# Loading q and k so that neighbouring partitions hold neighbouring token pairs

## The chip, the cores and the metric

The kernel runs on one core of one Trainium2 chip. The metric is the device time of one execution in microseconds (us), and the median over the runs is compared. A core has five engines with queues of their own: PE (TensorE, matrix products), DVE (VectorE), ACT (ScalarE), POOL (GpSimd) and SP (SyncE, which here only issues transfers). Each engine works through its own instructions in order. Sixteen DMA engines move data between the device memory and the on-chip memory of 128 partitions.

## The reference

The program is sliding-window attention followed by a gated feed-forward layer:

```
q, k, v: [8 batches, 8 heads, 576 tokens, 64]   float32
scores = q k^T / 8 + bias,  bias = -slope[h] * |i - j|,  only 0 <= i - j < 128
attn   = softmax(scores);   a = attn v
x      = a as [4608 tokens, 512]
H = max(x w_h, 0);  T = sigmoid(x w_t + b_t)
out    = T * H + (1 - T) * x                     [4608, 512] float32
```

## The kernel before

**Tiles.** A batch has eight heads in two groups `g` of four. Its 576 tokens go through four stages `s` of 128 queries; the last 64 tokens of two batches share a fifth block. The first half of the program is attention: for each batch and group, q and k are loaded (`load`, L150), transposed on DVE (`tr`, L231), multiplied on PE (`scores`, L263), put through the exponential on ACT (`soft`, L277), multiplied by a mask on DVE (`mask`, L283 to L287) and multiplied by v on PE (`pv`, L309). `norm` (L319, L320) on DVE divides by the sums. The second half takes the result `x` of a block, transposes it on PE (L329), copies it (L334), multiplies it by the two weight matrices (L347, L386), and forms the gate: `uu` (L356), tanh (L398), scaling of `tt` on ACT or DVE (L406, L408), the products and sums of L364, L417 and L424 on POOL or DVE, and the store on SP (L430).

**The load of q and k.** For batch `b`, group `g` and kind q or k, one transfer issued by POOL brings four heads of 576 tokens into the tile `LD[b % 2, g, kind]`, 128 partitions of 18 x 64 bf16, and casts from float32 on the way. The pattern is `"h (s t) d -> (h s) (t d)"` with t = 18: partition 32h + s holds tokens 18s to 18s + 17 of head h, one run of 4608 bytes in the device memory and of 2304 on the chip. There are 32 such loads, two sets of tiles in turn, so that a load of batch b + 2 comes behind the transpose of batch b in the same tile. v has a load per batch (L156) of 4608 pieces of 64 values, and SP copies half of v across partitions (`vo`, L172). Where the profile writes `ld11k`, the first digit is `b % 2`, the second `g`.

**The transpose.** DVE's transpose works on blocks of 32 x 32. A token's 64 bf16 values are read as 32 words of 4 bytes, so one block is 32 partitions by one token index t: it reads 32 words of one token index from each partition, and writes, into a partition per word, 32 values that lie 18 words (72 bytes) apart. Its output tile `TR` has, in partition 32h + i, word i of every token of head h in token order, and `scores` reads the even and the odd value of each word through its last index `e`.

**The order.** The program's order is a string, ORDER, of three-character steps, a letter for the function and two digits for the place in its list (`lists()`); each engine's queue has its steps in that order. `L` is a load of q or k, `T` a transpose, `V` a load of v, `G`, `g`, `o` and `O` the gates and adds on POOL and DVE. On POOL the loads of q, k and v stand between gates (L417) and adds (L424), and an issue takes POOL's own time. A transpose waits for its load, an issue on POOL waits for the transpose that last read its tile, and an issue waits for an earlier transfer with the same semaphore, of which POOL has eight in turn.

Of the kernel before, what the change touches and what calls it, by code (L numbers as in the profile page):

```python
# [9 lines left out]
P = 128  # L10
NB, NS, NG, NH = 8, 4, 2, 4
NP, NP3, NT, NVO = 5, 3, 18, 4
SPIN = 22
FILL = {(0, 1): 2, (0, 2): 2, (0, 3): 2, (1, 0): 2, (1, 1): 2}
SIG = {(3, 4), (7, 0), (7, 1), (7, 2), (7, 3)}
# [58 lines left out]
def kernel(  # L74
# [10 lines left out]
    nc = tc.nc  # L85
    B, H, S, D = q.shape
# [6 lines left out]
    U32 = mybir.dt.uint32  # L93
# [18 lines left out]
    LD = {(i, g, w): cp.tile([P, NT * D], BF16, name=f"ld{i}{g}{w}")  # L112
          for i in range(2) for g in range(NG) for w in "qk"}
    TR = {(i, g, w): cp.tile([P, SQ, 2], BF16, name=f"tr{i}{g}{w}")
          for i in range(2) for g in range(NG) for w in "qk"}
# [23 lines left out]
    def between(ins, last=None):  # L139
        last = last or paired[0]  # L140
        if last is not None:
            tc.add_manual_dep(
                ins.ins, last.name,
                mybir.DependencyInfo(mybir.DependencyClass.Sync, mybir.DependencyReason.DATA),
                reason="starts behind an operation of VectorE")

    def load(kind, *at):
        if kind in "qk":
            b, g = at
            nc.gpsimd.dma_start(  # L150
                out=LD[b % 2, g, kind][:],
                in_=(q if kind == "q" else k)[b, 4 * g : 4 * g + 4].rearrange(
                    "h (s t) d -> (h s) (t d)", t=NT))
        elif kind == "v":
            b, = at
            ins = nc.gpsimd.dma_start(  # L156
                out=va[:, b, :, 0:D],
                in_=v[b].rearrange("h s d -> (h s) d").rearrange("(n p) d -> p n d", p=P))
            if scaled[0] is not None:
                between(ins, scaled[0])  # L160
        elif at[0] < 2:
            nc.gpsimd.dma_start(
                out=(wH, wT)[at[0]][:],
                in_=(moe_w_h, moe_w_t)[at[0]].rearrange("(c p) n -> p c n", p=P))
        else:
            nc.gpsimd.dma_start(
                out=bT[0:1, :], in_=moe_b_t.rearrange("(o n) -> o n", o=1))
# [60 lines left out]
            nc.scalar.copy(out=MK[:, :, 1, 192:256], in_=MK[:, :, 0, 0:D])  # L228

    def tr(w, b, g):  # L230
        ins = nc.vector.transpose(  # L231
            out=TR[b % 2, g, w][:, 0:S].rearrange("p s e -> p (s e)").bitcast(U32).rearrange(
                "p (s t) -> p t s", t=NT),
            in_=LD[b % 2, g, w][:].bitcast(U32).rearrange("p (t i) -> p t i", i=32))
        if b == 0:
            turned[0] = ins.ins

    def warm():
        ps = take(1)[:, 0, :]
        for _ in range(SPIN):  # L240
            nc.tensor.matmul(out=ps, lhsT=spin[:, 0:P], rhs=spin[:], start=True, stop=True)
# [4 lines left out]
    def take(n, dtype=F32):  # L246
        i = int(next(bank))
        t = PS[:, i : i + n, :]
        return t if dtype == F32 else t.bitcast(dtype)
# [163 lines left out]
    def gate(b, s, on, half=0):  # L413
        eng, note = (nc.vector, alone) if on == "g" else (nc.gpsimd, between)
        at = cols(b, s, half)
        uu = UU[b, s][:, at]
        note(eng.tensor_tensor(out=uu, in0=uu, in1=TT[b, s][:, at], op=ALU.mult))  # L417

    def add_x(b, s, on, half=0):
        eng, note = (nc.gpsimd, between) if on == "o" else (nc.vector, alone)  # L420
        if half == 0:
            OT[b, s] = op.tile([P, DM], F32, name="ot")
        at = cols(b, s, half)
        note(eng.tensor_tensor(out=OT[b, s][:, at], in0=UU[b, s][:, at], in1=X[b, s][:, at], op=ALU.add))  # L424

    def store(b, s, half=0):
# [5 lines left out]
        for r in range(2):  # L432
# [5 lines left out]
                  q=lambda b, s, half: gate(b, s, "g", half), j=lambda b, s, half: add_x(b, s, "O", half))  # L438

    do = dict(L=load, V=load, W=load, X=lambda w, b: across(b), b=bias, T=tr, s=scores, e=soft, m=mask, p=pv, n=norm, x=x_tr, c=x_copy, h=mm_h,  # L440
              u=relu_sub, v=sub_x, z=mm_z, a=tanh, t=to_gate, g=gate, o=add_x, d=store)
    with tc.manual_schedule():
        steps = "".join(ORDER)
        for n in range(0, len(steps), 3):
# [19 lines left out]
            kind = step.lower() if step in "GOU" else {"D": "t", "N": "v"}.get(step, step)  # L464
# [30 lines left out]
```

## Time and profile before

| | |
|---|---|
| median of 3 runs | 153.02 us (151.66 to 153.88) |
| profiled execution | 151.17 us |
| its span, first to last instruction | 149.5 us |
| TensorE clock granted | 0.995 |
| PE busy | 121.4 us (81%) |
| DVE busy | 130.8 us (88%) |
| ACT busy | 120.6 us (81%) |
| POOL busy | 93.2 us (62%) |
| the 32 transposes of q and k (L231) | 4 x (5.0 us) for each of 8 tiles, 1241 to 1252 ns each in the mean |
| issue of the 32 loads of q and k (L150) | 551 to 618 ns of POOL each in the mean |
| packets of the software queue | 42688, 15.21 MB |
| packets in all | 49403, under 512 bytes 38496 |

The profile is of one execution. Busy times add up the instructions of an engine. A line of a group gives source line, engine, operation, output and input, shapes, count, then busy time and mean of one in ns, then the idle time of the engine just before them and what ended it. A line of the order in time gives start, duration, engine, source line and tiles. The waits name who waited for whom, with total, number and longest. Windows give each engine's busy time in a stretch of the span.

### The profile page before, as it was taken

To read this page: it belongs to the slowest core of one execution; us is meant where nothing else is said; L and a number is where in the kernel's file an instruction comes from. 1 tells how busy PE (TensorE), PEld (TensorE's weight loads), DVE (VectorE), ACT (ScalarE), POOL (GpSimd) and SP (SyncE) were. 2 spreads that over 40 slices of the span, in tenths; PEclk is the share of its full clock that TensorE was granted. 3 is DMA by queue.
4 is the path that set the end of the run, shared out by engine and by line. 5 is a ranking of instruction groups with operands and counts; after the bars stand their busy time and mean duration, and the time that the engine had idled before them with its cause. 6 is when DMAs were issued, how large, how long until landed. Compare 5 with 4: busy or idle time off the path is not lost.

```text
span 149.5 us, 6187 instructions
## 1 busy us (share of the span) xinstructions
PE 121.4 (81%) x2680; PEld 68.7 (46%) x2713; DVE 130.8 (88%) x248; ACT 120.6 (81%) x177; POOL 93.2 (62%) x101
## 2 busy tenths in 40 slices
PE   0008897887999897979999699968999999999940
PEld 0003544364555454554565455444555645556420
DVE  3687499997999999999999899299999999999990
ACT  3085907858799999979999899959999999999720
POOL 6990700089098986996999953918699933609030
PEclk9999999999999999999999999999999999999997
DMA  2999999999999999999979999988927996350752
GB/s 38 196 164 181 216 232 186 169 152 200 162 181 197 243 167 198 224 257 177 213 236 174 201 167 271 267 154 223 186 105 133 144 295 177 136 151 7 274 219 71
DMA packets 49403, 27.44 MB, mean 184 GB/s; under 512 B 38496, under 2 KB 39776, under 8 KB 49376
## 3 DMA queue, kind: packets, MB, share of 16 engines
q0 software_dynamic: 42688, 15.21, 96.9%
q1 hardware_dynamic: 6528, 11.71, 23.6%
q8 instruction: 21, 0.34, 1.0%
q10 hardware_dynamic: 160, 0.13, 0.3%
q14 instruction: 6, 0.05, 0.1%
HBM read 30.41 MB, written 9.44 MB: 267 GB/s over the span
## 4 chain that ended last, share of the span: by engine, by line
DMA 42%; DVE 21%; ACT 12%; POOL 7%; issue 7%; PE 6%; SPq 1%; DVEq 0%; POOLq 0%
DMA va<-in_v_dram 24%; DMA ld01k<-in_k_dram 10%; DMA vo<-va 7%; DVE x L320 5%; DVE uu L356 3%; ACT p L277 3%; POOL uu L417 2%; DVE p L283 2%; ACT tt L398 2%; PE ps L386 2%; ACT e L277 2%; ACT xt L334 2%; DVE ot L424 2%; DVE tr01q L231 2%; POOL ot L424 2%
## 5 line engine op out<-in xcount | busy, mean ns | idle before, releaser
L424 POOL TENSOR_TENSOR ot<-uu,x 128x512 f32<-128x512 bf16 x29 | 33.1, 1157 | 16.3 <-DVE uu L417 6.0
L277 ACT ACTIVATE p<-ps 128x1536 bf16<-128x1536 f32 x24 | 34.9, 1461 | 7.7 <-PE ps L263 7.4
L386 PE MATMUL ps<-wT,xt 128*128 128x512 bf16 x128 | 35.9, 380 | 1.3 <-ACT ps L377 0.3
L417 POOL TENSOR_TENSOR uu<-uu,tt 128x512 bf16<-128x512 bf16 x17 | 19.5, 1151 | 26.8 <-DVE tt L408 13.8
L347 PE MATMUL ps<-wH,xt 128*128 128x512 bf16 (+1 forms) x134 | 35.2, 373 | 1.1 <-issue 0.5
L320 DVE TENSOR_TENSOR x<-ps,rd 128x512 bf16<-128x512 f32 x36 | 24.9, 692 | 1.8
L283 DVE TENSOR_TENSOR p<-p,mk 128x1536 bf16<-128x1536 bf16 x24 | 22.5, 949 | 0.5 <-ACT p L277 0.4
L334 ACT COPY xt<-ps 128x512 bf16<-128x512 bf16 x36 | 21.2, 596 | 1.6 <-PE ps L329 1.6
L398 ACT ACTIVATE tt<-ps 128x512 f16<-128x512 f32 x31 | 18.6, 616 | 3.3 <-PE ps L386 2.7
L309 PEld LDWEIGHTS <-p 64*128 64x128 bf16 x768 | 15.2, 94 | 12.6 <-issue 11.2
L309 PE MATMUL ps<-vo,p 64*128 64x65 bf16 x384 | 17.8, 191 | 3.2 <-DMA vo<-va 2.6
L309 PE MATMUL ps<-va,p 64*128 64x65 bf16 x384 | 18.3, 191 | 1.6 <-DVE uu L356 1.4
L356 DVE SCALAR_TENSOR_TENSOR uu<-ps,x 128x512 bf16<-128x512 f32 (+1 forms) x29 | 19.1, 662 | 0.5 <-PE ps L347 0.5
L377 ACT COPY ps<-bA 128x512 f32<-128x512 f32 x32 | 19.3, 608 | 0.1
L347 PEld LDWEIGHTS <-xt 128*128 128x128 bf16 x148 | 12.7, 98 | 12.3 <-issue 1.1
L386 PEld LDWEIGHTS <-xt 128*128 128x128 bf16 x144 | 12.6, 98 | 12.3 <-issue 0.9
L263 PE MATMUL ps<-tr00q,tr00k 32*64 32x192 bf16 (+1 forms) x288 | 10.0, 254 | 10.1 <-DVE tr00k L231 9.6
L156 POOL DMA_DIRECT2D va<-in_v_dram x8 | 14.8, 1849 | 4.5 <-DMA va<-in_v_dram 4.0
L329 PE MATMUL ps<-ident,x 128*128 128x128 bf16 x144 | 13.6, 220 | 2.4 <-DVE x L320 1.4
L277 ACT ACTIVATE e<-ps 128x1792 bf16<-128x1792 f32 x8 | 13.3, 1667 | 2.4 <-PE ps L263 2.3
L263 PEld LDWEIGHTS <-tr00k 32*64 32x64 bf16 x288 | 6.7, 108 | 15.6 <-DVE tr00k L231 9.6
L329 PEld LDWEIGHTS <-x 128*128 128x128 bf16 x144 | 9.6, 97 | 9.0 <-issue 3.6
(79 smaller groups left out, 213.8 us busy)
## 6 DMA issues: line engine op xcount, KB each, us to landing
out_dram<-ot SPq DMA_DIRECT2D x32, 256.0 KB, 4.0
va<-in_v_dram POOLq DMA_DIRECT2D x8, 576.0 KB, 11.1
vo<-va SPq DMA_DIRECT2D x16, 146.2 KB, 5.8
ld00q<-in_q_dram POOLq DMA_DIRECT2D x4, 288.0 KB, 7.2
ld01k<-in_k_dram POOLq DMA_DIRECT2D x4, 288.0 KB, 5.7
ld00k<-in_k_dram POOLq DMA_DIRECT2D x4, 288.0 KB, 6.7
ld01q<-in_q_dram POOLq DMA_DIRECT2D x4, 288.0 KB, 7.3
ld11k<-in_k_dram POOLq DMA_DIRECT2D x4, 288.0 KB, 7.4
```

Source lines behind the costliest of these rows:

```text
L277: nc.scalar.activation(out=out, in_=in_, func=ACTF.Exp, scale=scale)
L283: alone(nc.vector.tensor_tensor(out=p, in0=p, in1=MK[:, :, :, 0:192], op=ALU.mult))
L309: nc.tensor.matmul(out=av[o : o + m, g, h * (D + 1) : (h + 1) * (D + 1)], lhsT=PT[bb, st][rows, h].rearrange("p i n -> p (i n)")[:, c : c ...
L320: nc.vector.tensor_tensor(out=x[:].rearrange("p (r i d) -> p r i d", i=NH, r=2), in0=av[:, :, :, 0:D], in1=rd[:].to_broadcast([P, 2, NH, D ...
L329: nc.tensor.transpose(out=pt[:, c * P : (c + 1) * P], in_=X[b, s][:, c * P : (c + 1) * P], identity=ident[:])
L334: nc.scalar.copy(out=xt[:].rearrange("p c n -> p (c n)"), in_=XP.pop((b, s)))
L347: nc.tensor.matmul(out=pa, lhsT=XT[b, s][:, c, :], rhs=wH[:, c, at], start=c == 0, stop=c == NC - 1)
L356: nc.vector.scalar_tensor_tensor(out=uu, in0=pa, scalar=0.0, in1=X[b, s][:, at], op0=ALU.max, op1=ALU.subtract)
L386: nc.tensor.matmul(out=pz, lhsT=xt[:, c, :], rhs=wT[:, c, :], start=c == 0 and not given, stop=c == NC - 1 and given, skip_group_check=given)
L398: nc.scalar.activation(out=tt[:], in_=pz, func=ACTF.Tanh, scale=0.5)
L417: note(eng.tensor_tensor(out=uu, in0=uu, in1=TT[b, s][:, at], op=ALU.mult))
L424: note(eng.tensor_tensor(out=OT[b, s][:, at], in0=UU[b, s][:, at], in1=X[b, s][:, at], op=ALU.add))
```

## The change

For batches 2 to 7 (FLAT = 2) the load and the transpose get other patterns; batches 0 and 1 keep the old ones. A token index is now split as 36a + 4c + 2j + e, with 64 values of a over the four heads, nine of c, and two each of j and e. Partition 2a + j holds the nine pairs (c; e = 0, 1), so neighbouring partitions hold neighbouring pairs of tokens. Each pair is a run of 512 bytes in the device memory and 256 on the chip. The load becomes two transfers, one for the even partitions (j = 0) and one for the odd ones (j = 1), each of 64 partitions x 9 runs. The transpose reads as before, 32 words of one token index (c, e) from each of 32 partitions, but writes them along a (36 words apart) and j (2 words apart): two words for each a, 8 bytes apart, in one aligned run of 16 bytes. The output tile holds the same values in the same places as before. Scores, the order and all else are unchanged.

```diff
+FLAT = 2
...
         if kind in "qk":
             b, g = at
-            nc.gpsimd.dma_start(
-                out=LD[b % 2, g, kind][:],
-                in_=(q if kind == "q" else k)[b, 4 * g : 4 * g + 4].rearrange(
-                    "h (s t) d -> (h s) (t d)", t=NT))
+            src = (q if kind == "q" else k)[b, 4 * g : 4 * g + 4]
+            if b < FLAT:
+                nc.gpsimd.dma_start(
+                    out=LD[b % 2, g, kind][:],
+                    in_=src.rearrange("h (s t) d -> (h s) (t d)", t=NT))
+            else:
+                src = src.rearrange("h s d -> (h s) d").rearrange(
+                    "(a c j e) d -> j a c (e d)", c=NT // 2, j=2, e=2)
+                for j in range(2):
+                    nc.gpsimd.dma_start(
+                        out=LD[b % 2, g, kind][j::2].rearrange("a (c x) -> a c x", c=NT // 2),
+                        in_=src[j])
...
     def tr(w, b, g):
+        out = TR[b % 2, g, w][:, 0:S].rearrange("p s e -> p (s e)").bitcast(U32)
+        if b < FLAT:
+            out = out.rearrange("p (s t) -> p t s", t=NT)
+        else:
+            out = out.rearrange("p (a c j e) -> p c e a j", c=NT // 2, j=2, e=2)
         ins = nc.vector.transpose(
-            out=TR[b % 2, g, w][:, 0:S].rearrange("p s e -> p (s e)").bitcast(U32).rearrange(
-                "p (s t) -> p t s", t=NT),
-            in_=LD[b % 2, g, w][:].bitcast(U32).rearrange("p (t i) -> p t i", i=32))
+            out=out, in_=LD[b % 2, g, w][:].bitcast(U32).rearrange("p (t i) -> p t i", i=32))
```

In the new kernel the load of batches 0 and 1 is line 153 and that of batches 2 to 7 line 160.

## The prediction, written before the run

> **What bounds the kernel now.** I read the page first (busy time by engine, and the chain of work that ended last), then the busy time by stage in windows, then the groups by line and shape, then the order of time on POOL around the q and k loads.
>
> ```profile
> PE 121.4 (81%) x2680; PEld 68.7 (46%) x2713; DVE 130.8 (88%) x248; ACT 120.6 (81%) x177; POOL 93.2 (62%) x101
> ...
> DMA 42%; DVE 21%; ACT 12%; POOL 7%; issue 7%; PE 6%; SPq 1%; DVEq 0%; POOLq 0%
> ```
>
> DVE is the busiest engine, POOL looks free by a third, and the chain runs through loads for 42% of the span. An average hides where POOL is free, so the next view is by stage:
>
> ```profile
> core 0: us, PE busy (x) PEld busy (x) DVE busy (x) ACT busy (x) POOL busy (x), PEclk, DMA share, GB/s
> 31.00:48.00 17.00, 15.51 (x373) 8.98 (x383) 15.70 (x26) 14.71 (x21) 12.24 (x15) 1.00 1.40 176
> 48.00:65.00 17.00, 14.52 (x327) 8.76 (x331) 16.50 (x28) 16.68 (x26) 14.90 (x15) 1.00 1.47 217
> 65.00:82.00 17.00, 16.32 (x395) 9.34 (x400) 16.47 (x27) 15.76 (x22) 15.64 (x16) 1.00 1.50 203
> 82.00:99.00 17.00, 14.05 (x292) 7.85 (x296) 13.55 (x25) 16.07 (x27) 11.02 (x12) 1.00 1.63 229
> 99.00:113.00 14.00, 13.38 (x359) 7.72 (x358) 13.72 (x25) 12.36 (x17) 10.19 (x11) 1.00 0.71 152
> ```
>
> From 31 to 82 us DVE is busy 48.67 of 51 us and POOL 42.78 of 51: POOL has 8.2 us free where the loads of batches 3 to 6 are issued, and what it has free after 113 (15.88 busy of 36.5) comes too late for any load of q or k. Issuing is POOL's own time:
>
> ```profile
> L156 POOL DMA_DIRECT2D va<-in_v_dram x8 | 14.8, 1849 | 4.5 <-DMA va<-in_v_dram 4.0 <-issue 0.5
> L150 POOL DMA_DIRECT2D ld01k<-in_k_dram x4 | 2.3, 574 | 0.0
> L162 POOL DMA_DIRECT2D wH<-in_moe_w_h_dram x1 | 0.8, 785 | 0.0
> L166 POOL DMA_DIRECT2D bT<-in_moe_b_t_dram x1 | 0.6, 573 | 0.0
> ```
>
> The mean of one issue grows with its pieces: 573 ns for bT (16 pieces, by its pattern), 574 for a q or k load (128 rows), 785 for wH (512), 1849 for v (4608). And the loads are used soon after they land:
>
> ```profile
> 67.24 0.61 POOL L150 DMA_DIRECT2D ld11k<-in_k_dram  x1
> 67.84 0.54 POOL L150 DMA_DIRECT2D ld00k<-in_k_dram  x1
> 68.36 0.55 POOL L150 DMA_DIRECT2D ld11q<-in_q_dram  x1
> ```
> ```profile
> 74.00 1.25 DVE L231 STREAM_TRANSPOSE tr11k<-ld11k 128x576 uint32<-128x576 uint32 x1
> ```
>
> POOL issues back to back; this ld11k (batch 5) lands at 73.22 by the trace and is transposed 0.8 us later. By the same reading ld11k of batch 3 has 0.02 us to spare, ld01k of batch 6 0.02, the q and k of heads 0 to 3 of batch 2 0.28 and 0.61, most others 1.4 to 8.
>
> **The change, part by part.**
>
> *Transposes.* 24 of 32 keep their 576 columns and get another output walk. Rows for the price:
>
> ```profile
> L231 DVE STREAM_TRANSPOSE tr00k<-ld00k 128x576 uint32<-128x576 uint32 x4 | 5.0, 1247 | 0.0
> L424 DVE TENSOR_TENSOR ot<-uu,x 128x512 f32<-128x512 bf16 x6 | 4.0, 685 | 0.0
> L424 DVE TENSOR_TENSOR ot<-uu,x 128x256 f32<-128x256 bf16 x2 | 0.8, 418 | 0.0
> L189 DVE MEMSET va<- 128x288 bf16 x1 | 0.3, 298 | 1.0 <-issue 1.0
> L176 DVE MEMSET bT<- 128x256 uint32 x1 | 0.3, 272 | 0.0
> ```
>
> The adds that write dense 4-byte columns take 685 - 418 = 267 ns for 256 columns, 1.04 ns each, plus 151 fixed. At that rate 576 columns cost 752 ns; the transpose takes 1247, or 1.90 ns a column. If its 72-byte output step is the reason, the change saves up to 0.50 us each, 24 x 0.50 = 12 us of DVE time. The other end is nothing: the memset of L189 steps 130 bytes between elements and takes 298 ns for 288, on the line of the dense ones (165 for 128, 272 for 256, so 299 for 288). A loss is not excluded, the walk now has four dimensions; I bound it by 0.1 us each (2.4 in all). I take 0.50, since an operation that also reads is nearer to the adds than to a memset, and keep both ends.
> The Trainium skill, SBUF — State Buffer, section "Door 1", says that SBUF has 16-byte lines and that two accesses to a line are needed for full rate. By it the saving is real, by the memset row it is nil; the sum below moves by only 1 us between them.
>
> *Issue on POOL.* 24 loads become 48, each of 64 x 9 = 576 pieces. Between wH (512, 785 ns) and v (4608, 1849) the line gives 0.80 us. A load then costs 2 x 0.80 - 0.575 = +1.03 us of POOL. Ends: flat at 0.575 each (+0.575), and 0.85 (+1.13); below nothing only if the price went with the 64 partitions, and bT on one partition costs as much as 128. I take +1.03. Two of the loads (16.8 and 17.3) stand before a 12.4 us wait of POOL and cost it nothing. The order counted from the list of issues is 8 loads in 31 to 48, 4 in 48 to 65, 4 in 65 to 82, 6 in 82 to 113. What stands behind them on POOL, in order, are the gates of L417, the adds of L424, the v loads and the next q and k loads.
>
> The ledger for POOL, 31 to 82: 42.78 + 16 x 1.03 = 59.3 us of work in 51. So POOL, with no gap at all, is 8.3 us late at 82. The loads there have 0.02 to 1.4 us to spare, so DVE waits for them, and with it PE's scores and all behind. DVE's 16 transposes of that stretch, 8 us shorter, give nothing back: DVE waits instead. From 82 to 113 POOL has 21.21 + 6 x 1.03 = 27.4 us of work in 31, and DVE 8 transposes left (4.0 us saved), but ACT is busy 28.43 of those 31; I let it win back 0.8 us. Without faster transposes it wins back none: 1 us, as said. Sum: +7.5 us.
>
> *Transfers.* In the trace's packets 1229 to 1237 of 128 bytes start each us while v flows alone, 90 to 94 of 2304 bytes: 13 and 178 ns per packet on one of 16 engines. The line between gives 22.7 ns for the new 256-byte packets. A load was 8 x 178 = 1.42 us and becomes 2 x 36 x 22.7 = 1.63: +0.2 us, 5 us in all, inside the time that POOL's lateness opens between loads; I cost it at nothing. If that cover is gone, up to 0.2 x 16 = 3.3 us by 82.
>
> *Waits.* In the kernel's list of instructions POOL's transfers signal on eight semaphores in turn, so each issue waits for the eighth transfer before it. It shows once:
>
> ```profile
> POOL va L156 <- DMA va<-in_v_dram: 4.0, 1, 4.0
> ```
>
> With 67 transfers instead of 43 that comes more often. Eight issues of 0.80 us are 6.4 us; a load lands in 5.7 to 7.8 (medians), a v load in 11.1. I cost it at nothing where POOL is late anyway, and at 4 us for the upper end. Each transpose waits for two transfers, the second 0.80 us after the first; this is in the +1.03. PE, ACT and SP keep their instructions.
>
> The Trainium skill, DMA: Bandwidth & Descriptors, section "Rules for kernel authors", speaks against the split: two transfers to disjoint halves of the partitions serialize, and one of 128 is to be used. By it alone a load would cost one more fixed issue (+0.575); the rows above already hold that.
>
> **The rivals.**
>
> - *The issue is flat.* The piece count is nothing, two issues cost 1.15 us. For it: bT and q/k at 573 and 574. Against: wH and v. Ledger: 42.78 + 16 x 0.575 = 52.0 of 51, +1.0 by 82, little won back: 152 to 155. The Trainium skill says in DMA: Bandwidth & Descriptors, "Anatomy of one DMA", that descriptor generation is small and many fit before its cost shows; that is this rival, and the v row at 1849 ns disagrees.
> - *Faster: the issue goes with the partitions.* A half then costs 0.29, a load as much as now, and the 12 us of DVE time come free. It decides from an extra of under 0.33 us per load: 42.78 + 16 x 0.33 = 48, 3 us under 51. ACT (82.4 busy in 30 to 120) and PE (81.6) would stop it after some 8 us; I take -5, 148 us. Against: bT.
> - *More waits.* The eighth-transfer wait comes on top (+4): 164.5.
> - *The change does nothing on DVE.* Transposes stay at 1247 and POOL's ledger stays: 161.5. It is inside the forecast's range.
>
> **How the numbers follow.** The profiled execution took 151.17 us (span 149.5 and 1.7 around it); the median of the runs, 153.02, is 1.85 above it. +7.5 gives 158.7 against the profiled one and 160.5 by the median; I give 160.5. Chances: POOL's issue time is the bound, transposes shorter or not, 0.66; more waits 0.14; flat issue 0.13; faster 0.07. So slower by over 2% is 0.80, within 2% 0.13, faster 0.07; 2% is about what runs from 151.66 to 153.88 can tell from no change. The forecast's own range is 156.5 to 163. The range for 8 in 10 is 155 to 165: it leaves out the faster case (0.07), most of the flat one (0.08) and the worst waits (0.05).
>
> **What would show it.** In the profile after: issues of L160 at about 0.80 us, 48 of them, and 16 of L153 as now; POOL busy 93.2 + 24 x 1.03 = 118 us and nearly all of 31 to 90; DVE idle before transposes of ld tiles, 8 us and more where it was 0.3 + 2.6 after 31 us; the transposes of batches 2 to 7 at 0.75 us, those of 0 and 1 at 1.25; packets 49403 - 24 x 128 + 48 x 576, about 74000, with the software queue's share little changed. Wrong it would be if an issue took under 0.45 us, if POOL kept free time from 31 to 82, or if DVE's waits for the loads did not grow.

## The result and the profile after

The changed kernel took 161.81 us (median of 4, 160.97 to 162.13) against 153.45 (median of 4, 151.66 to 155.27): a ratio of 1.058 with a 95% interval of 1.047 to 1.069. The profiled execution took 160.97 us, its span 159.2. Ratios here leave out executions that were disturbed by a lower granted clock, medians keep them, so that the two do not always divide exactly. All executions of the kernel before, in the rounds of the experiments too, took 151.10 to 158.19 us, less than the shortest of the changed kernel.

The page of the changed kernel, busy times:

```profile
PE 127.1 (80%) x2713; PEld 70.1 (44%) x2713; DVE 133.3 (84%) x248; ACT 121.3 (76%) x177; POOL 118.4 (74%) x125
...
DMA packets 74364, 27.45 MB, mean 172 GB/s; under 512 B 66528, under 2 KB 67808, under 8 KB 74336
...
q0 software_dynamic: 67648, 15.21, 111.3%
```

POOL went from 93.2 to 118.4 us. DVE did not become lighter, although its transposes did (below). There are 385 packets more than the 73979 of the prediction's sum; e3 below, which has the 24 transfers more but no new pieces, also has 385 more than the kernel before. The software queue's packets took 111.3% of the span of 16 engines instead of 96.9%.

The windows of the changed kernel, with the same columns as before (length, PE, PEld, DVE, ACT, POOL, clock, DMA):

```profile
31.00:48.00 17.00, 16.38 (x384) 9.41 (x384) 14.16 (x26) 14.55 (x21) 16.73 (x19) 1.00 1.68 154
48.00:65.00 17.00, 13.41 (x330) 8.14 (x331) 13.51 (x21) 13.55 (x20) 16.94 (x16) 0.90 1.71 185
65.00:82.00 17.00, 13.87 (x307) 7.66 (x306) 13.42 (x21) 12.65 (x19) 16.96 (x18) 1.00 1.54 156
82.00:99.00 17.00, 13.73 (x268) 7.67 (x269) 15.67 (x26) 14.14 (x22) 16.86 (x16) 0.90 2.01 190
```

POOL is busy 50.63 of the 51 us from 31 to 82, and full on to 99. In these 51 us every other engine is busy for less time: DVE is busy 41.09 of the 51 us where it was busy 48.67. What POOL does there is read from the groups and from the order of time on POOL:

```profile
L165 POOL DMA_DIRECT2D va<-in_v_dram x8 | 14.7, 1837 | 4.2 <-DMA va<-in_v_dram 4.2
L160 POOL DMA_DIRECT2D ld10k<-in_k_dram x6 | 4.6, 773 | 0.0
```
```profile
74.79 1.55 POOL L160 DMA_DIRECT2D ld11k<-in_k_dram  x2
76.34 1.50 POOL L160 DMA_DIRECT2D ld00k<-in_k_dram  x2
77.83 1.50 POOL L160 DMA_DIRECT2D ld11q<-in_q_dram  x2
```
```profile
111.76 0.59 POOL L150 DMA_DIRECT2D ld11q<-in_q_dram  x1
```
```profile
121.03 1.55 POOL L160 DMA_DIRECT2D ld11q<-in_q_dram  x2
```

An issue takes 756 to 773 ns in the mean of each tile, two of them 1.5 us. The three loads whose issue took from 67.24 to 68.91 us now take from 74.79 to 79.33; the last load of all (the last two views, before and after) is issued at 121.03 instead of 111.76, 9.3 us late, and the span is 9.7 us longer. The lateness at the last load is carried to the end.

DVE around 70 us, in order of time, in the kernel before with its groups for the mask and for POOL's gate, then DVE and POOL in the changed kernel:

```profile
69.81 1.25 DVE L231 STREAM_TRANSPOSE tr10k<-ld10k 128x576 uint32<-128x576 uint32 x1
70.91 0.68 DVE L356 SCALAR_TENSOR_TENSOR uu<-ps,x 128x512 bf16<-128x512 f32 x1
```
```profile
L283 DVE TENSOR_TENSOR p<-p,mk 128x1536 bf16<-128x1536 bf16 x24 | 22.5, 949 | 0.5 <-ACT p L277 0.4
L417 POOL TENSOR_TENSOR uu<-uu,tt 128x512 bf16<-128x512 bf16 x17 | 19.5, 1151 | 26.8 <-DVE tt L408 13.8
```
```profile
69.48 0.77 DVE L245 STREAM_TRANSPOSE tr01q<-ld01q 128x576 uint32<-128x576 uint32 x1
...
71.93 1.90 DVE L295 TENSOR_TENSOR p<-p,mk 128x1536 bf16<-128x1536 bf16 x1
73.76 1.50 DVE L298 TENSOR_TENSOR r<-e,mk 128x768 bf16<-128x768 bf16 x1
75.18 0.68 DVE L299 TENSOR_TENSOR r<-e,mk 128x1024 bf16<-128x1024 bf16 x1
75.78 0.77 DVE L245 STREAM_TRANSPOSE tr10k<-ld10k 128x576 uint32<-128x576 uint32 x1
76.48 0.65 DVE L368 SCALAR_TENSOR_TENSOR uu<-ps,x 128x512 bf16<-128x512 f32 x1
```
```profile
71.82 1.19 POOL L436 TENSOR_TENSOR ot<-uu,x 128x512 f32<-128x512 bf16 x1
72.98 1.86 POOL L429 TENSOR_TENSOR uu<-uu,tt 128x512 bf16<-128x512 bf16 x1
```

The new walk takes 0.77 us instead of 1.25. The records of neighbouring DVE operations overlap a little, so the order of time gains less than the 0.48: the next operation starts 1.10 us after the start of an old transpose and 0.70 after that of a new one, which is 0.40 for each and 9.6 for 24. But the mask product, 0.95 us before, takes 1.90 here, and the next 1.50 instead of 0.55: they run while POOL, behind its time, does an add and a gate, and the gate is stretched too (1.86 for 1.15). Counted over the trace, 16 of the bf16 products of DVE and 3 of its scalings of `tt` are over a quarter longer than the shortest of their kind while a POOL product or add runs; before there were 2. Against the shortest, these groups lost 13.8 us, before 1.9: 11.9 us more, against the 9.6 us that the transposes gave back. The difference is about the 2.5 us by which DVE's busy time grew.

DVE's waits for loads after 31 us and for PE at `uu` in the kernel before, and its longest waits in the changed kernel:

```profile
DVE tr01k L231 <- DMA ld01k<-in_k_dram: 2.6, 1, 2.6
DVE uu L356 <- PE ps L347: 0.5, 2, 0.3
DVE tr11k L231 <- DMA ld11k<-in_k_dram: 0.3, 1, 0.3
```
```profile
DVE uu L368 <- PE ps L359: 4.2, 4, 1.5
DVE uu L368 <- POOL ot L436: 3.0, 1, 3.0
DVE tr11k L245 <- DMA ld11k<-in_k_dram: 2.8, 1, 2.8
DVE tr10q L245 <- DMA ld10q<-in_q_dram: 2.1, 1, 2.1
DVE tr00q L245 <- DMA ld00q<-in_q_dram: 1.6, 1, 1.6
```

The wait for ld11k, at 49.5 us, is for batch 3, whose load had 0.02 us to spare in the kernel before; the last two lie in the first 18 us. After 31 us DVE waits 3.5 us for loads (2.8 at 49.5, 0.3 at 51.4, 0.5 at 105.1), where it waited 2.9 before: hardly more. What grew are the waits for POOL's add (3.0 and one of 0.4, none before) and for PE at `uu` (4.2 instead of 0.5). Two of the latter, 1.5 us at 58.7 and 1.1 us at 89.1, end shortly after the two stretches of halved clock that the last section names. Of the 9.7 us of longer span, 2.5 are DVE's busy time and 7.2 its idle time.

### The profile page after: what moved, and what is told of

Same layout as the page of the kernel before. It is cut to its first block, busy times and chain, and to the rows that moved or that the text cites. A ratio compares the mean times of both kernels' runs of the same rounds, so it can differ in the third digit from the quotient of the medians.

```text
span 159.2 us, 6266 instructions
## 1 busy us (share of the span) xinstructions
PE 127.1 (80%) x2713; PEld 70.1 (44%) x2713; DVE 133.3 (84%) x248; ACT 121.3 (76%) x177; POOL 118.4 (74%) x125
## 3 DMA queue, kind: packets, MB, share of 16 engines
q0 software_dynamic: 67648, 15.21, 111.3%
q1 hardware_dynamic: 6528, 11.71, 22.8%
## 4 chain that ended last, share of the span: by engine, by line
DVE 24%; DMA 23%; POOL 21%; PE 19%; issue 7%; ACT 3%; SPq 0%; DVEq 0%; POOLq 0%
DMA ld01k<-in_k_dram 7%; DMA va<-in_v_dram 6%; POOL ot L436 5%; DVE p L295 5%; DMA ld01q<-in_q_dram 5%; POOL uu L429 5%; PE ps L359 4%; DVE x L332 4%; DVE uu L368 4%; DMA vo<-va 3%; PE ps L275 3%; PE ps L253 3%; POOL va L165 3%; PE ps L398 3%; PE ps L321 3%
## 5 line engine op out<-in xcount | busy, mean ns | idle before, releaser
L436 POOL TENSOR_TENSOR ot<-uu,x 128x512 f32<-128x512 bf16 x29 | 34.3, 1195 | 12.8 <-DVE uu L429 5.9
L398 PE MATMUL ps<-wT,xt 128*128 128x512 bf16 x144 | 37.3, 383 | 3.9 <-ACT ps L389 3.9
L359 PE MATMUL ps<-wH,xt 128*128 128x512 bf16 (+1 forms) x148 | 37.7, 380 | 0.0
L429 POOL TENSOR_TENSOR uu<-uu,tt 128x512 bf16<-128x512 bf16 x17 | 20.7, 1223 | 14.0 <-DVE tt L420 9.9
L295 DVE TENSOR_TENSOR p<-p,mk 128x1536 bf16<-128x1536 bf16 x24 | 26.7, 1123 | 0.5 <-ACT p L289 0.4
L332 DVE TENSOR_TENSOR x<-ps,rd 128x512 bf16<-128x512 f32 x36 | 24.9, 692 | 2.0 <-POOL ot L436 0.4
L321 PE MATMUL ps<-vo,p 64*128 64x65 bf16 x384 | 18.4, 193 | 2.6 <-DMA vo<-va 1.6
L398 PEld LDWEIGHTS <-xt 128*128 128x128 bf16 x144 | 12.9, 98 | 16.3 <-issue 5.1
L359 PEld LDWEIGHTS <-xt 128*128 128x128 bf16 x148 | 13.1, 99 | 12.8 <-issue 1.8
L341 PE MATMUL ps<-ident,x 128*128 128x128 bf16 x144 | 14.2, 227 | 4.5 <-DVE x L332 3.4
```

The lines of the kernel that those rows point to most:

```text
L295: alone(nc.vector.tensor_tensor(out=p, in0=p, in1=MK[:, :, :, 0:192], op=ALU.mult))
L321: nc.tensor.matmul(out=av[o : o + m, g, h * (D + 1) : (h + 1) * (D + 1)], lhsT=PT[bb, st][rows, h].rearrange("p i n -> p (i n)")[:, c : c ...
L332: nc.vector.tensor_tensor(out=x[:].rearrange("p (r i d) -> p r i d", i=NH, r=2), in0=av[:, :, :, 0:D], in1=rd[:].to_broadcast([P, 2, NH, D ...
L341: nc.tensor.transpose(out=pt[:, c * P : (c + 1) * P], in_=X[b, s][:, c * P : (c + 1) * P], identity=ident[:])
L359: nc.tensor.matmul(out=pa, lhsT=XT[b, s][:, c, :], rhs=wH[:, c, at], start=c == 0, stop=c == NC - 1)
L398: nc.tensor.matmul(out=pz, lhsT=xt[:, c, :], rhs=wT[:, c, :], start=c == 0 and not given, stop=c == NC - 1 and given, skip_group_check=given)
```

## The experiments

Three theories. *POOL's time*: the issues make POOL full from 31 to 99 us, and all that hangs on its order comes late. *Packets*: the 256-byte pieces, or the second transfer of a load, are slow. *Collisions*: the DVE time lost beside POOL's late operations is what costs. "Changed" and "before" name the two kernels of the diff.

**e1: the new loads with the old walk.**

```diff
-        if b < FLAT:
-            out = out.rearrange("p (s t) -> p t s", t=NT)
-        else:
-            out = out.rearrange("p (a c j e) -> p c e a j", c=NT // 2, j=2, e=2)
+        out = out.rearrange("p (s t) -> p t s", t=NT)
```

> The loads of the change with the old output walk of the transposes (the tokens land in another order, so the output differs). Issue theory (POOL's 25 us of extra issue time set the pace): POOL about 118 us busy, transposes 1.25 us, time 161 to 165, within 2% of the changed kernel, since the faster transposes were hidden. Collision theory (late gates and adds on POOL run into DVE's fast bf16 operations and eat the 11 us saved on the transposes): nothing pays for the collisions now, DVE busy 140 or more, time 167 to 172. Packet theory (the 256-byte packets land late): as the changed kernel, 161 to 162, with DVE waiting for loads.

Measured 161.33 us (158.84 to 163.37), ratio 1.049 (1.028 to 1.070): the changed kernel's time without its faster transposes. The loss comes with the loads, and what the walk saves is not seen beside them: the intervals of the two kernels overlap. DVE was 140.6 us busy, 7.3 more than in the changed kernel, and the time stayed: DVE's busy time is not what sets the end here, against the collision theory.

**e2: the old loads with the new walk.**

```diff
-            if b < FLAT:
+            if True:
                 nc.gpsimd.dma_start(
                     out=LD[b % 2, g, kind][:],
```

> The old loads, one transfer each, with the new output walk of the transposes for batches 2 to 7 (the tokens land in another order, so the output differs). Issue and collision theory alike: POOL 93 us, issues 0.575 us, 24 transposes at 0.77 us, DVE busy about 119 to 120, masks at 0.95 us, time 145 to 150. If ACT and PE set the pace once DVE is quicker: 151 to 154. If it stays at 160, the loads were not the cause at all.

Four executions took 149.40, 153.28, 154.00 and 155.39 us, too few and too far apart for a ratio. Their median, 153.64, is 0.6 us under that of the kernel before in the same rounds (154.26), and the shortest is 1.7 us under its shortest (151.10). The profile is of the execution of 153.28 us. There the transposes take 0.77, the masks 961 ns in the mean, and DVE is 123.5 us busy, 7.3 less than before, but it waits elsewhere:

```profile
DVE rd L331 <- PE ps L321: 6.7, 6, 3.3
DVE uu L368 <- PE ps L359: 3.2, 6, 0.9
```
```profile
PE ps L321 <- DMA vo<-va: 5.0, 2, 2.8
```

In this execution PE and the transfer of v come next. So the DVE time that the new walk saves seems worth little even where nothing takes it away: between nothing and some 2 us, which these four executions do not settle.

**e3: two transfers per load, long rows, old walk.**

```diff
-                src = src.rearrange("h s d -> (h s) d").rearrange(
-                    "(a c j e) d -> j a c (e d)", c=NT // 2, j=2, e=2)
+                src = src.rearrange("h (s t) d -> (h s) (t d)", t=NT)
                 for j in range(2):
-                    nc.gpsimd.dma_start(
-                        out=LD[b % 2, g, kind][j::2].rearrange("a (c x) -> a c x", c=NT // 2),
-                        in_=src[j])
+                    nc.gpsimd.dma_start(out=LD[b % 2, g, kind][j::2], in_=src[j::2])
...
```

> Each load of batches 2 to 7 in two transfers of 64 partitions (even, odd), each partition still one run of 2304 bytes; old walk; same result as before. Two issues per load without the many pieces. Issue theory: 0.575 us each, POOL 93 + 24 x 0.575 = 107 us, time 154 to 158. Packet theory: the packets are those of before, so 153 within 1%. Price by partitions (a half costs half): POOL 93, time 153.

Measured 154.54 us (151.25 to 158.03, 10 executions), ratio 1.002 (0.993 to 1.012): no change that shows. The issues take 554 to 571 ns in the mean of each tile, for 64 rows about what 128 take, so the price is not by partitions, and POOL is busy 105.9 us. The second transfer as such costs 1.2% at most; 12.7 us more of POOL are nearly or wholly covered.

**e4: one transfer per load, cut into 256-byte pieces.** The tile gets a gap of 16 bytes after each 256, which the transpose (old walk) skips.

```diff
+PITCH = 136
...
+                nc.gpsimd.dma_start(
+                    out=LD[b % 2, g, kind][:].rearrange("p (c x) -> p c x", x=PITCH)[:, :, 0 : 2 * D],
+                    in_=src.rearrange("h (s c e) d -> (h s) c (e d)", c=NT // 2, e=2))
...
```

> Each load of batches 2 to 7 in one transfer of 128 partitions, cut into nine pieces of 256 bytes per partition by a tile with a gap of 16 bytes after each; tokens and walk as before, same result. The same number of 256-byte packets as the changed kernel, half the issues. Issue theory: 1152 pieces cost about 0.95 us, POOL 93 + 24 x 0.38 = 102 us, time 153 to 157. Packet theory: 160 to 162 as the changed kernel. If the pieces cost nothing to issue: 0.575 us and 153.

Measured 154.58 us (153.94 to 156.29), ratio 1.015 (0.997 to 1.033). The page of e4:

```profile
DMA packets 73979, 27.44 MB, mean 180 GB/s; under 512 B 66144, under 2 KB 67424, under 8 KB 73952
...
q0 software_dynamic: 67264, 15.21, 116.0%
```
```profile
L158 POOL DMA_DIRECT2D ld01k<-in_k_dram x3 | 3.1, 1022 | 0.0
```

These are the 256-byte packets of the changed kernel, with an even larger share of the DMA engines, and the loss is 1.5%, at the upper end of the interval 3.3%, where the change cost 5.8%: the packets are not the main cause. A small part is not excluded by this run. The issue of 1152 pieces takes 1.02 us, POOL is 103.5 us busy.

**e5 and e6: without POOL's 17 gate products**, from the changed kernel (e5) and from the one before (e6).

```diff
+            if step == "G":
+                continue
             if step in second:
```

> The changed kernel without the 17 gate products that POOL does (they are left out, so the output differs). The loads, their 48 issues and their packets stay. POOL-time theory: POOL 118 - 21 = 97 us, which is under the 104 to 106 that two transfers or many pieces alone left harmless, so the time falls to 149 to 153 and the masks go back to 0.95 us. Packet theory: 159 to 162, as the changed kernel.

> The control for the run above: the kernel before without the same 17 gate products on POOL. POOL-time theory: POOL 93 - 20 = 73 us; POOL had time to spare, so little comes of it: 150 to 153. If the products cost the kernel before as much as the changed one, 145 or less, and then the run above says nothing about the loads.

Measured: e5 157.15 us (154.99 to 159.75), ratio 1.022 (1.013 to 1.030), e6 156.70 (155.15 to 157.73). With 20 us less on POOL, the new loads cost nothing to be seen: the two lie 0.5 us apart. But neither expectation of a level held. The control is slower than the kernel before, ratio 1.027 (1.018 to 1.037), with POOL at 73.6 us and the masks at 949 ns. In e6 DVE waits 8.1 us for PE at the division, and PE 5.6 us for v's copy across partitions, where before these were 2.0 and 2.6:

```profile
PE ps L309 <- DMA vo<-va: 5.6, 2, 3.2
```

Why PE then waits longer for v's copy was not tried, so the pair says what the loads cost beside a lighter POOL, and no more. They also show that less POOL time need not make this kernel faster.

**e7 and e9: the kernel before with an idle fill on POOL behind each load of batches 2 to 7**, 768 columns (e7) and 1040 (e9). Loads, transfers, packets and transposes are those of before.

```diff
...
+            if b >= 2:
+                nc.gpsimd.iota(idle[:], pattern=[[1, IDLE]], base=0, channel_multiplier=-1)
```

> The kernel before, loads and transposes untouched, with one idle index fill on POOL (768 columns, about 1 us, its output is not used) behind each of the 24 loads of batches 2 to 7. POOL-time theory: POOL about 118 us, full from 31 to 99, time 158 to 163, masks over 1.0 us in the mean. Packet theory, and the theory that the second transfer of a load is what hurts: 152 to 154.

> As the run with the idle fill of 768 columns behind each of the 24 loads, but with 1040 columns: POOL 93 + 24 x 1.06 = 117 to 118 us, the amount of the changed kernel, with the packets and transfers of before. POOL-time theory: 160 to 163. Theory that a third of the loss comes from the second transfers or the packets: 157 to 159. Packet theory: 153.

Measured: e7 158.86 us (155.81 to 160.67), ratio 1.030 (1.019 to 1.041), POOL 110.9 us and not the 118 that was expected, since a fill took 0.79 us; e9 162.82 (160.69 to 164.15), ratio 1.051 (1.040 to 1.062), POOL 116.2. The page and the fills of e9:

```profile
PE 130.6 (80%) x2713; PEld 71.3 (44%) x2713; DVE 141.2 (87%) x248; ACT 121.6 (75%) x177; POOL 116.2 (72%) x125
```
```profile
L158 POOL IOTA idle<- 128x1040 int32 x24 | 24.5, 1019 | 0.2
```

24.5 us of POOL time at the places of the loads, with no change to any transfer, give the loss of the changed kernel within its interval, and of e1. This is the strongest run for POOL's time. The fill by itself does not slow the masks: the four that run beside a fill, and beside no gate or add of POOL, take 0.93 to 0.95 us.

POOL's busy time over the whole run does not order the runs: e12 below has 106.0 us, like e3, and costs 2.4%. Its lateness near 82 us goes together with the loss, among the runs that add POOL time at the loads. The add of POOL that starts at 78.85 us in the kernel before starts 2.0 us later in e3 and e4 (0.2% and 1.5%), 5.3 in e7 (3.0%), 8.1 in e9 (5.1%), 8.7 in e1 (4.9%) and 9.2 in the changed kernel (5.8%).

**e10: the collisions taken away.** In the changed kernel every mask product and scaling of `tt` waits for the POOL operation that precedes it in the program.

```diff
...
+    def behind(ins):
+        if late[0] is not None:
+            between(ins, late[0])
...
+            behind(ins)
             alone(ins)
```

> The changed kernel with one more wait: each mask product and each scaling of tt on DVE starts behind the gate, subtraction or add that stands before it for POOL in the program's order. The collisions then can't happen, the loads stay. Theory that the collisions are the cost (13 us of DVE time): masks at 0.95 us, time 150 to 155. Theory that POOL is simply late and the collisions are where it shows: DVE waits for POOL instead, 160 to 167.

Measured 160.42 us (159.87 to 161.16), ratio 1.045 (1.038 to 1.051). DVE is 123.5 us busy, 9.8 less than in the changed kernel, and the masks are back:

```profile
L301 DVE TENSOR_TENSOR p<-p,mk 128x1536 bf16<-128x1536 bf16 x24 | 22.5, 953 | 4.1 <-POOL ot L452 2.6 <-POOL uu L442 1.1 <-ACT p L295 0.4
L306 DVE TENSOR_TENSOR r<-e,mk 128x768 bf16<-128x768 bf16 x8 | 4.4, 553 | 3.0 <-POOL uu L442 1.6 <-POOL ot L452 1.4
L432 DVE TENSOR_SCALAR tt<-tt 128x512 f16<-128x512 f16 x11 | 3.3, 300 | 3.1 <-POOL ot L452 1.7 <-POOL uu L442 1.3
```

The time hardly moves: the collisions have become waits for POOL. By the medians it is worth 1.4 us to shut them out (161.81 - 160.42), with intervals that overlap. A wait can be as long as the stretch that it replaces, so this run alone does not price the collisions. Together with e1, where DVE was 7.3 us busier in the same time, it points to them as the place where the lateness shows, rather than a cost of their own.

**e8: both groups in one transfer, from the kernel before.** Tried as a way to lighten POOL.

```diff
...
+            if b >= 2:
+                if g == 0:
+                    nc.gpsimd.dma_start(
+                        out=LM[b % 2, kind][:],
+                        in_=(q if kind == "q" else k)[b].rearrange(
+                            "(g h) (s t) d -> (h s) g (t d)", g=NG, t=NT))
+                return
...
```

> The kernel before with both groups of heads in one transfer for batches 2 to 7 (12 transfers of 256 rows for 24 of 128, into tiles of their own, issued where group 0 was loaded; old walk; same result). POOL-time theory: 93 - 12 x 0.5 = about 87 us; POOL had time to spare, so 150 to 154, no change to tell. If POOL's load issues cost the kernel before something already: 146 to 150.

Measured 156.43 us (153.60 to 157.36), ratio 1.018 (1.003 to 1.032): slower, where 150 to 154 was expected, with POOL at 88.6 us. A load of both groups lands 8.4 to 10.9 us after its issue (medians of each tile), one of the loads before 5.7 to 7.8. In the profiled execution of 157.04 us DVE waits 3.8 us once for a load of both groups and 3.9 for PE. The lighter POOL came with later loads, so the run does not tell what POOL's issues cost the kernel before.

**e11 and e12: the changed kernel with POOL's gate products on DVE**, all 17 (e11) or every second (e12).

```diff
+            if step == "G":
+                step = "g"
             kind = step.lower() if step in "GOU" else {"D": "t", "N": "v"}.get(step, step)
```

> The changed kernel with the 17 gate products of POOL done by DVE at the same place in the program's order (same result). POOL 118 - 20 = 98 us, DVE 133 - 13 (no collisions) + 17 x 0.43 = 127 us. POOL-time theory: 150 to 155, about the kernel before. Packet theory: 159 or more.

> The changed kernel with every second of POOL's 17 gate products done by DVE (9 of them, same result). POOL 118 - 10 = 107 us, DVE about 125 to 128. POOL-time theory: POOL as busy as with two flat transfers, which cost nothing, so 150 to 156. Packet theory: 159 or more.

Measured: e11 155.65 us (153.58 to 158.95), ratio 1.008 (1.003 to 1.013); e12 156.84 (155.77 to 158.68), ratio 1.024 (1.017 to 1.032), POOL 106.0 us. Both medians lie just above what was expected. The page of e11:

```profile
PE 126.3 (82%) x2713; PEld 69.6 (45%) x2713; DVE 129.0 (84%) x265; ACT 120.9 (79%) x177; POOL 96.4 (63%) x108
```

With the 48 issues and all the packets of the change in place, giving DVE POOL's gate products takes back 6 of the 8.4 us. That it is the faster transposes which make room for them on DVE is not shown: no run has these gates on DVE with the old walk. Neither run beats the kernel before, and none of the others is shown to.

## Why the prediction was right, point by point

- *The issue on POOL* was taken at 0.80 us and measured 0.76: with 0.575 for the old load, 2 x 0.764 - 0.575 = +0.95 per load instead of +1.03, 22.9 us in all. POOL's own products and adds grew by 2.3 us in the collisions, which makes up the 25.2. The ends were right to be kept: 64 rows alone cost 0.565 (e3).
- *The ledger* said that POOL has 59.3 us of work for the 51 from 31 to 82 and is 8.3 late. It was busy 50.63 of 51, and the load of q for batch 6, heads 0 to 3, was issued at 89.12 instead of 79.95, 9.2 late:

```profile
79.95 0.61 POOL L150 DMA_DIRECT2D ld00q<-in_q_dram  x1
```
```profile
89.12 1.55 POOL L160 DMA_DIRECT2D ld00q<-in_q_dram  x2
```

  That it came so near is in part luck. With the measured price it gives 42.78 + 16 x 0.95 = 58.0, 7.0 late; the other 2.0 us are POOL's gates and adds of that stretch, which the collisions made longer and for which the sum had no term. A price that was 1.3 us too high in all stands against it.
- *The gain back from 82 to 113* was taken at 0.8 us. There was none: 9.2 late at 89, 9.3 at 121. This term was off by its whole size, 0.8 of the 7.5.
- *The way from POOL to DVE* was wrong in its main part. The prediction said that the loads from 31 to 82 us have 0.02 to 1.4 us to spare, and let DVE wait for them, "8 us and more" where it was 2.9. Its own reading ahead of that sum says "most others 1.4 to 8", and in the trace before, 12 of these 16 loads have 1.7 to 8.1 us between landing and transpose. DVE's waits for loads after 31 us grew to 3.5 us only, close to the prediction's own sign of being wrong. POOL's lateness reached DVE by way of its gates and adds instead: collisions with them (11.9 us more than before, against the 9.6 saved), waits for POOL's add (3.4), and waits for PE at `uu` (3.7 more). The sum did not notice, since it went by POOL's ledger; e10 fits this, as the same time comes back as waits for POOL when the collisions are shut out.
- *The transposes* were taken at 0.75 us and measured 0.77, so the adds' rate was the right end and the memset row the wrong one; of the 0.48 us, 0.40 are gained in the order of time, 9.6 us in all where 12 was the sum. The 16-byte rule of the Trainium skill, SBUF — State Buffer, section "Door 1", agrees with the trace for the output of a transpose: one word per run 1.25 us, two words 0.77. That it changes the sum by only 1 us fits: e1 and the changed kernel cannot be told apart.
- *Transfers* at nothing: e4 leaves room for a little (1.5%, with 10 us more on POOL in the same run), and e9 has the loss without them. The share of the software queue rose by 14 points, where the prediction let it change little. The price of a packet was right where they flow fastest: at most 702 of 256 bytes start in a us, 22.8 ns each on one of 16 engines, priced at 22.7.
- *The eighth-transfer wait* was priced at up to 4 us: POOL waited 1.4 us more, once, at 21 us, where it had time. That rival fell.
- *The flat issue* fell with 1.02 us for 1152 pieces (e4). The sentence of the Trainium skill, DMA: Bandwidth & Descriptors, section "Anatomy of one DMA", that descriptor generation is small does not hold for this kernel's POOL.
- *The split* into two transfers, against which the Trainium skill speaks (DMA: Bandwidth & Descriptors, section "Rules for kernel authors"), cost nothing to be seen by itself (e3).

## What to carry to other kernels

Make the sum for the engine that issues the transfers, by stage, and not by its share of the span: POOL had 38% free, and the stage in which it was needed had 16%. A price per transfer becomes a loss where the free time of that stage ends: 10 and 13 us more cost 1.5% and 0.2% (e4, e3), 25 us cost 5 to 6%. Lateness of the issuing engine need not show as waits for the loads; look at everything else that stands behind the issues in its queue. A saving on the busiest engine is worth only what the next waits leave of it, so first run the saving alone, as e2 tried to, and only then pay for it.

## What the runs showed of the hardware

- The DVE products of two bf16 tiles in on-chip memory take longer beside a POOL product or add (0.95 to 1.90 us, 0.55 to 1.50), and the POOL operation can be stretched with them (1.15 to 1.86). Operations that read PE's output (L332, 0.69 us) and the transposes show no such change. The Trainium skill, SBUF — State Buffer, section "Who interferes with whom", says that a DVE instruction with two such inputs contends with a POOL instruction that reads there; the trace agrees.
- An issue on POOL took 0.565 us for 64 rows, 0.575 for 128, 0.764 for 576 pieces, 1.02 for 1152 and 1.84 for 4608. The two-group load of e8, 256 long rows, took 0.74 to 0.76 in the mean of each tile, so pieces alone do not give the price.
- In several runs the granted clock fell to half for stretches of 3.4 us in the middle: twice in the profiled execution of the changed kernel (from 53.7 and from 84.4 us), not in that of the kernel before. In e2 it fell at 38.8 us, shortly after PE had waited for v's copy. That the gaps of PE bring it about fits, but no run here tries it; it may account for a part of the spread of the times and of e5 and e6. It is not what makes the changed kernel slow: e9 took 160.69 us in an execution with a granted clock of 0.995, which has no room for such a stretch, and the kernel before 151.10 with 0.998.
